# A paced feed-forward fill beside attention, and layers of neighbour jobs in turns behind it

## The chip, the cores and the metric

The kernel runs on one core of one Trainium2 chip. A core has five engines that run beside one another, each through its own list of instructions in order: TensorE (PE in the profile: matrix products, and transposes done as products), VectorE (DVE), ScalarE (ACT), GpSimd (POOL), and SyncE (SP), which here only issues DMAs. They wait for one another through semaphores. The metric is the device time of one execution in microseconds (us); lower is better.

## The reference

Masked attention on 8 batches of 8 heads with 576 positions of width 64, and behind it a feed-forward network on all 4608 tokens (512 wide, 2048 hidden):

```
scores = (1/8) * q @ k^T                      # 64 heads, 576x576
scores = where(scores >= rowmax - tau, scores, -1e9)
attn   = exp(scores - rowmax) / (sum + 1e-9)
x      = attn @ v                             # -> 4608 x 512
h      = x @ w_in                             # 512 -> 2048
g      = max(h, 0) + alpha * min(h, 0)
out    = g @ w_out                            # 2048 -> 512
```

The weights are float64, and single precision is wanted. So each operand is cut into a high part that TensorE takes whole and a low part with the rest, and a product is made of three (high by high, high by low, low by high).

## The kernel before

**Attention.** 32 pairs of heads, each cut into nine units (128 queries of a head; the fifth unit holds the rest of both heads). The main loop (L992) takes one unit a *cycle*, 288 cycles in all. In cycle i, PE makes the scores of unit i+2 (`s`, L423) and transposes the masked weights of unit i (`t`, `tk`, L467 and L483); DVE masks unit i (`p`, L458), takes the low part of a transposed unit (L523), and finds the row maxima of unit i+2 (`nmx`, L438); ACT makes exponentials and high parts. In four cycles of nine PE also multiplies weights by values (`av`, L570). A score tile has two homes in PSUM, so the scores of unit i+2 wait until unit i is masked. The finished x goes to DRAM (`xs`).

**The fill.** Feed-forward work is put into the same cycles. The first six of the 16 hidden chunks (`fcs1`) are done for *groups* of 256 tokens, 18 groups in all. A group's x is loaded and split (L698 to L705), then come six first-layer steps (L1 in this text: 12 products, `pha`), each followed a cycle later by the activation (L225 to L237), and then 36 second-layer products (L2, `acca`), which go into `part`. `Mlp.cycle` decides from a credit: each cycle adds `CYCLE` less the cycle's planned attention work, an L1 takes 1.31 and an L2 0.216, in planned microseconds. An L1 is let in while the credit is above `TH1` and the cycle has no `av`, an L2 while it is above `TH2`. Group x has one home, and a group's load enters the queue `l1` only behind the last L1 of the group before.

**Behind attention** (`behind`, L798). What is left of the groups becomes jobs of kind a; then nine jobs of 512 tokens for chunks 6 to 9 (kind b, `phb`, `accb`), then nine for chunks 10 to 15 (kind c, `phc`, `accc`). `order` lists whole steps: `step1` is one chunk's first layer, `step2` the whole second layer of 128 tokens. Between two jobs comes one `step1` of the next job, all `step2` of the last, then the other `step1`. x is loaded into `homexr` at the first step of the job before, and split in four quarters, one a step: ACT makes `homexh` (L868), DVE `homexl` (L869). Weights of later chunks are decoded from their float64 words in eight small steps each (`decode`, L826), among them POOL's product (L844) and its `join` (L162, recorded at L168).

All engine lists but SP's are in the order in which this code writes them.

Of the kernel before, what the change touches and what calls it, by code (L numbers as in the profile page):

```python
# [35 lines left out]
GB = 10  # L36
# [14 lines left out]
XO = 1  # L51
L2O = 3
P1 = 2
# [7 lines left out]
CYCLE = 2.6  # L61


def f(ap):
    return ap.bitcast(F32)
# [10 lines left out]
def tile_masked_attention_moe(  # L76
# [558 lines left out]
    def at_cycle(i, fn, *a):  # L635
        later.setdefault(i, []).append((fn, a))
# [44 lines left out]
    class Mlp:  # L681


        def __init__(self):
            self.l1, self.l2 = deque(), deque()
            self.acc = None
            self.live = 0
            self.gap = 0
            self.room = 0.0

        def ready(self, gi):
            t0, n = groups1[gi]
            st = {"g": {}}
            self.l1.append((gi, st, None))
            for i in range(F1):
                self.l1.append((gi, st, i))

        def step_l1(self, i):  # L698
            gi, st, fi = self.l1.popleft()
            t0, n = groups1[gi]  # L700
            if fi is None:
                st["xr"] = load_x(mem.mp1, t0, n, G1, 1)
                at_cycle(i + XO, lambda: st.update(x=split_x(mem.mp1, st["xr"], t0, n, G1, 1)))
                self.gap = i + XO + 2
                return  # L705
            name = f"a{gi}_{fi}"
            self.live += 1
            ph = layer1(ps_m, fcs1[fi], n, st["x"], name)

            def act(ph=ph):  # L710
                st[fi] = prelu1(mem.mp1, G1, fcs1[fi], n, ph, name, 2)
                prelu2(*st[fi], n)

            def spl():
                g = mem.mp1.tile([P, 2, G1], F32R, tag="g", name=f"g{name}", bufs=GB)
                split_g(g, st.pop(fi)[0], n, dict(p=nc.gpsimd, v=nc.vector).get(SPG))
                st["g"][fi] = g

            at_cycle(i + ACTO, act)
            at_cycle(i + SPLO, spl)  # L720
            if fi == F1 - 1:
                for o in range(0, n, P):
                    for fj in range(F1):
                        self.l2.extend((i + L2O, gi, st, o, fj, ti) for ti in range(3))

        def step_l2(self, i):
            _, gi, st, o, fj, ti = self.l2.popleft()
            t0, n = groups1[gi]
            m = min(P, n - o)
            if fj == 0 and ti == 0:  # L730
                self.acc = ps_m.tile([P, 512], F32, tag="pm", name=f"acca{gi}_{o}")
            acc = self.acc
            layer2(acc, fcs1[fj], st["g"][fj], o, m, fj == 0, fj == F1 - 1, (ti,))
            if ti < 2:
                return
            if o + P >= n:
                self.live -= 1
            if fj == F1 - 1:

                def put():  # L740
                    po = mem.mp1.tile([P, DM], F32, tag="po", name=f"po{gi}_{o}", bufs=1)
                    nc.scalar.activation(po[:m], acc[:m], AF.Copy)
                    nc.sync.dma_start(part[gi][o : o + m, :], po[:m])

                first_at_cycle(i + PUTO, put)

        def cycle(self, i, used, slot):

            self.room = min(self.room, TH3) + CYCLE - used
            l1 = False  # L750
            if self.l1 and i >= self.gap and self.live < GB:
                if self.l1[0][2] is None:
                    self.step_l1(i)
# [3 lines left out]
            while self.l2 and self.l2[0][0] <= i and self.l2[0][4] in self.l2[0][2]["g"] and ("o", fcs1[self.l2[0][4]]) in ready and self.room > TH2:  # L757
                self.step_l2(i)
                self.room -= 0.216
            return l1  # L760
# [37 lines left out]
    def behind():  # L798
# [5 lines left out]
        while mlp.l2 and (mlp.l2[0][4], mlp.l2[0][5]) != (0, 0):  # L804
            mlp.step_l2(10**6)
# [43 lines left out]
        class Job:  # L849


            def __init__(self, fcs, t0, n, gn, kind):
                self.fcs, self.t0, self.n, self.gn, self.kind = fcs, t0, n, gn, kind
                self.g, self.x, self.todo = {}, None, list(range(len(fcs)))
                self.tiles = list(range(0, n, P))
                self.name = f"{kind}{t0}"
# [7 lines left out]
            def split(self, c):  # L864
                n = self.n
# [17 lines left out]
            def step2(self, o):  # L883
                m = min(P, self.n - o)
                t = self.t0 + o
                if self.kind != "a":
                    pin = wpool.b.tile([P, DM], F32, tag="pin", name=f"pin{self.name}_{o}", bufs=3)
                    gi, r = divmod(t, G1)
                    nc.sync.dma_start(pin[:m], part[gi][r : r + m, :] if self.kind == "b" else part2[t // P][:m])
                acc = ps_2.tile([P, 512], F32, tag="acc", name=f"acc{self.name}_{o}", bufs=4)  # L890
                nf = len(self.fcs)
                for i, fc in enumerate(self.fcs):
                    layer2(acc, fc, self.g[i], o, m, i == 0, i == nf - 1)
                if self.kind == "a":
                    po = mem.mp1.tile([P, DM], F32, tag="po", name=f"po{self.name}_{o}", bufs=1)
                    nc.scalar.activation(po[:m], acc[:m], AF.Copy)
                    gi, r = divmod(t, G1)
# [3 lines left out]
                nc.vector.tensor_tensor(ob[:m], acc[:m], pin[:m], op=ALU.add)  # L901
                nc.sync.dma_start(part2[t // P][:m] if self.kind == "b" else out[t : t + m, :], ob[:m])

        olds = {}
        for gi, st, o, fj, ti in [x[1:] for x in mlp.l2]:
            if ti == 0 and fj == 0:
                job = olds.get(gi)
                if job is None:
                    t0, n = groups1[gi]
                    job = olds[gi] = Job(fcs1, t0, n, G1, "a")  # L910
                    job.tiles, job.todo, job.g = [], [], st["g"]
                job.tiles.append(o)
        for gi, st, fi in mlp.l1:
            job = olds.get(gi)
            if job is None:
                t0, n = groups1[gi]
                job = olds[gi] = Job(fcs1, t0, n, G1, "a")
                job.todo, job.g = [], st["g"]
                if fi is not None:
                    job.x = st["x"]  # L920
            if fi is not None:
                job.todo.append(fi)
        first = [olds[gi] for gi in sorted(olds)]
# [14 lines left out]
        ahead = {}  # L938
        for a, b in zip(jobs, jobs[1:]):
            k = next(i for i, x in enumerate(order) if x[0] is a)  # L940
            ahead.setdefault(k, []).append(b)

        weights = [[decode(fc, io) for io in "io" for fc in fcs] for fcs in (fa, fb)]
        nsteps = [sum(x[0].kind == c for x in order) for c in "ab"]
        starts = {}
        at_ = 0
        for ws, n, (lo, hi) in zip(weights, nsteps, ((0.0, 0.78), (0.1, 0.85))):
            for i, w in enumerate(ws):
                k = at_ + n * (lo + (hi - lo) * i / max(1, len(ws) - 1))
                for j, fn in enumerate(w):  # L950
                    starts.setdefault(int(k) + j, []).append(fn)
            at_ += n

        xq = deque()
        for k, (job, what, i) in enumerate(order):
# [3 lines left out]
            for b in ([job] if k == 0 and what == 1 else []) + ahead.get(k, []):  # L959
                if b.x is None:  # L960
                    while xq:
                        a, c = xq.popleft()
                        a.split(c)
                    b.load()
                    xq.extend((b, c) for c in range(NCC))
            if what == 1:
                while xq and xq[0][0] is job:
                    b, c = xq.popleft()
                    b.split(c)
                job.step1(i)  # L970
            else:
                job.step2(i)
            for fn in starts.get(k, []):
                fn()
            if xq:
                b, c = xq.popleft()
                b.split(c)
# [110 lines left out]
```

## Time and profile before

| | us |
|---|---|
| runs without profile (3) | 1440.97, 1444.02, 1445.97 |
| median | 1444.02 |
| the profiled execution | 1436.55 |
| its span, first to last instruction | 1434.7 |

Busy time: PE 94% of the span (8008 products), DVE 73%, ACT 59%, POOL 50%. Products are pipelined and their ends are modelled, so a busy PE is not always at its peak; the distance from one product's start to the next is the better measure. Attention with the fill runs until about 834 us, the a jobs until about 932 us, b jobs to about 1126 us, c jobs to the end.

The score tiles name the cycles: pair 26 begins at 665.3 us, pair 27 at 690.6, pair 28 at 716.3 (the first product of each pair's unit 0), pair 7 at 178.7 and pair 31 at 792.7. "Cycle 0" of a pair below is the one in which PE makes the scores of its unit 0.

### The profile page before, as it was taken

The numbers are of one execution on the slowest core, as the hardware profiler recorded it, in microseconds if no ns is written. First come the engines' busy times: TensorE is split into PE (matmuls) and PEld (weight loads), VectorE is DVE, ScalarE is ACT, GpSimd is POOL, SyncE is SP. The second block draws the span as 40 slices with busy tenths as digits, with TensorE's granted clock in tenths as the row PEclk, the third lists the DMA queues.
The fourth block names the chain that finished last, engine by engine and source line by source line (L and its number), as shares of the span: only waits on it lengthen the run. The fifth ranks groups of instructions, "written<-read, shape, count | busy, mean of one in ns | idle before, by whom it ended". The sixth has DMA issues, their size and how long they took to land.

```text
span 1434.7 us, 23581 instructions
## 1 busy us (share of the span) xinstructions
PE 1352.4 (94%) x8008; PEld 1181.1 (82%) x8008; DVE 1046.0 (73%) x2044; ACT 841.6 (59%) x1909; POOL 710.7 (50%) x834
## 2 busy tenths in 40 slices
PE   6998999999999999999999979989999999999998
PEld 4656888998998898899889867768888888888887
DVE  7988988988888888888888828647777644444432
ACT  7887988888888888888888733323233211121110
POOL 3884764665755666565665525514444322222221
PEclk9999999999999999999999989999999999999999
DMA  7645454544545535445454133434654522223221
GB/s 227 185 127 148 126 138 131 144 135 135 144 128 144 140 106 162 126 119 155 121 144 121 33 120 113 140 119 150 209 178 157 176 89 89 88 88 103 100 68 61
DMA packets 113448, 186.01 MB, mean 130 GB/s; under 512 B 16593, under 2 KB 47601, under 8 KB 113329
## 3 DMA queue, kind: packets, MB, share of 16 engines
q1 hardware_dynamic: 113328, 184.51, 43.0%
q8 instruction: 64, 1.05, 0.3%
q14 instruction: 56, 0.45, 0.1%
HBM read 104.41 MB, written 37.90 MB: 99 GB/s over the span
## 4 chain that ended last, share of the span: by engine, by line
PE 79%; DVE 9%; ACT 5%; issue 4%; POOL 2%; DMA 1%; SPq 0%; POOLq 0%; ACTq 0%; DVEq 0%
PE av L570 11%; PE s L423 11%; PE accc L243 10%; PE phc L213 10%; PE acca L243 8%; PE pha L213 7%; PE accb L243 7%; PE t L467 7%; PE phb L213 6%; DVE p L458 2%; DVE nmx L438 2%; PE tk L483 1%; DVE eo L523 1%; ACT eo L519 1%; POOL ga L237 1%
## 5 line engine op out<-in xcount | busy, mean ns | idle before, releaser
L438 DVE TENSOR_REDUCE nmx<-s 128x1 f32<-128x576 f32 x288 | 216.5, 752 | 77.7 <-PE s L423 75.3
L458 DVE SCALAR_TENSOR_TENSOR p<-s,thr,p 128x576 f32<-128x576 f32 x256 | 206.8, 808 | 3.1 <-ACT thr L451 2.6
L243 PE MATMUL acca<-wo,ga 128*128 128x512 f32 x648 | 199.4, 425 | 6.2 <-ACT ga L234 4.4
L423 PE MATMUL s<-kh,qst 128*128 128x288 f32 x640 | 145.2, 317 | 58.4 <-DVE p L458 44.2
L446 ACT ACTIVATE p<-s,nmx 128x576 f32<-128x576 f32 x256 | 190.3, 743 | 9.9 <-DVE nmx L438 9.7
L237 POOL TENSOR_TENSOR gc<-ptc,gc 128x512 fp32r<-128x512 f32 x54 | 69.9, 1294 | 216.8 <-ACT gc L234 216.8
L234 ACT ACTIVATE gc<-ptc 128x512 fp32r<-128x512 f32 x54 | 34.1, 632 | 237.5 <-DVE ptc L878 237.5
L423 PEld LDWEIGHTS s<-kh,qst 128*128 128x128 f32 x640 | 100.4, 193 | 88.6 <-issue 52.4
L467 PE MATMUL t<-ident,p 128*128 128x128 f32 x1024 | 156.4, 276 | 0.0
L243 PE MATMUL accc<-wo,gc 128*128 128x512 f32 x648 | 148.5, 389 | 0.0
L243 PEld LDWEIGHTS accc<-wo,gc 128*128 128x128 f32 x648 | 121.5, 188 | 25.5 <-POOL gc L237 0.3
L243 PEld LDWEIGHTS acca<-wo,ga 128*128 128x128 f32 x648 | 117.1, 195 | 27.5 <-ACT ga L234 6.3
L213 PE MATMUL pha<-xh,wi 128*128 128x256 f32 x672 | 136.1, 285 | 0.3 <-ACT pra L226 0.3
L213 PE MATMUL phc<-homexh,wi 128*128 128x512 f32 x432 | 134.6, 389 | 0.0
L423 PE MATMUL s<-kl,qst 128*128 128x288 f32 x640 | 134.3, 300 | 0.0
L467 PEld LDWEIGHTS t<-ident,p 128*128 128x128 f32 x1024 | 127.6, 142 | 0.1
L213 PEld LDWEIGHTS pha<-xh,wi 128*128 128x128 f32 x672 | 109.8, 190 | 4.6 <-ACT pra L226 1.2
L237 POOL TENSOR_TENSOR ga<-pta,ga 128x256 fp32r<-128x256 f32 x108 | 82.9, 768 | 57.5 <-ACT ga L234 50.4
L570 PE MATMUL av<-eo,vst 128*128 128x322 f32 (+1 forms) x512 | 107.9, 334 | 0.0
L869 DVE TENSOR_TENSOR homexl<-homexr,homexh 128x512 fp32r<-128x512 f32 (+1 forms) x88 | 69.5, 793 | 50.1 <-ACT homexh L868 50.1
L523 DVE TENSOR_TENSOR eo<-t,eo 128x512 fp32r<-128x512 f32 (+1 forms) x168 | 97.3, 592 | 9.3 <-ACT eo L519 9.0
L423 PEld LDWEIGHTS s<-kl,qst 128*128 128x128 f32 x640 | 103.5, 193 | 0.0
(146 smaller groups left out, 3234.3 us busy)
## 6 DMA issues: line engine op xcount, KB each, us to landing
kr<-in_k_dram SPq DMA_DIRECT2D x31, 320.0 KB
rb<-rvd SPq DMA_DIRECT2D x64, 144.0 KB
xs<-xa SPq DMA_DIRECT2D x32, 288.0 KB
pinb<-part SPq DMA_DIRECT2D x36, 256.0 KB
part<-obb SPq DMA_DIRECT2D x36, 256.0 KB
pinc<-part SPq DMA_DIRECT2D x36, 256.0 KB
out_dram<-obc SPq DMA_DIRECT2D x36, 256.0 KB
vr<-in_v_dram SPq DMA_DIRECT2D x28, 320.0 KB
```

The costliest lines, as they stand in the source:

```text
L213: nc.tensor.matmul(ph[:, :n], w[:, c, :], xx[:, c, :n], start=(c == 0 and ti == 0), stop=(c == NCC - 1 and ti == 2),)
L234: nc.scalar.activation(g[:, 0, :n], t[:, :n], AF.Copy)
L237: nc.gpsimd.tensor_tensor(g[:, 1, :n], t[:, :n], f(g[:, 0, :n]), op=ALU.subtract)
L243: nc.tensor.matmul(acc[:m, :], gg[:, g, o : o + m], w, start=(first and ti == 0), stop=(last and ti == 2))
L423: nc.tensor.matmul(ps[:, h, :288], w, kk[:, a + h * 288 : a + (h + 1) * 288], start=(ki == 0 and i == 0), stop=(ki == 1 and i == n - 1),)
L438: nc.vector.tensor_reduce(self.nmx[:, j : j + 1], self.S[u][0][:, :, :288], axis=AX.XY, op=ALU.max, negate=True)
L446: nc.scalar.activation(pj, ps[:, :, :288], AF.Exp, bias=nmx[:, j : j + 1], scale=1.0)
L458: nc.vector.scalar_tensor_tensor(pj, ps[:, :, :288], thr[:, j : j + 1], pj, op0=ALU.is_ge, op1=ALU.mult, accum_out=self.sm[:, c : c + 1])
L467: nc.tensor.transpose(tb[:, c, :], pt[:, j, j * D + c * P : j * D + (c + 1) * P], ident)
L523: nc.vector.tensor_tensor(dst[1], ps, f(dst[0]), op=ALU.subtract)
L570: nc.tensor.matmul(pa[:m, :n], w, x, start=(part == 0 and c == 0), stop=(part == z.parts[-1] and c == NKC))
L869: nc.vector.tensor_tensor(xl[:, c, :n], xr[:, c, :n], f(xh[:, c, :n]), op=ALU.subtract)
```

## The change

Five things change.

1. x of a group is loaded up to a group ahead (`prefetch`), split three cycles after its load, into two homes.
2. L2 products are held back: while a group's L1 steps are under way, `keep` leaves a reserve of six L2 for each L1 that is still to come, less `SLACK`; and between groups a reserve that grows with the cycles until the next group is ready. An L1 may also enter an `av` cycle when the credit is above 1.2.
3. `CYCLE` falls from 2.6 to 2.44; `GB`, the number of homes for g, rises to 11.
4. Behind attention a `step2` is one chunk of one 128-token tile, and the steps of two neighbour jobs take turns by their share of the job (from a to b jobs they don't).
5. There the x quarters and the weight decode are set by a clock of planned step costs (`event`), and POOL makes `homexl`.

On PE, in the cycles with the scores of units 2 and 3 of pair 27 (`s27_2`, `s27_3`; `t` and `tk` are transposes, `av26` weights by values), before:

```order
L423 MATMUL s27_2_9924<-kh27_9486,qst1_111 128x288 x2
L423 MATMUL s27_2_9924<-kl27_9488,qst1_111 128x288 x2
L467 MATMUL t27_0_9931<-ident_60,p27_0_9886 128x128 x4
L423 MATMUL s27_3_9961<-kh27_9486,qst1_111 128x288 x2
L423 MATMUL s27_3_9961<-kl27_9488,qst1_111 128x288 x2
L467 MATMUL t27_1_9967<-ident_60,p27_0_9886 128x128 x4
L483 MATMUL tk27_0_9972<-ident_60,p27_0_9886 128x128
L243 MATMUL acca10_0_9974<-wo0_944,ga10_0_9411 128x512 x3
L243 MATMUL acca10_0_9974<-wo1_1041,ga10_1_9457 128x512 x2
```

The same two cycles now:

```order
L425 MATMUL s27_2_9862<-kh27_9399,qst1_111 128x288 x2
L425 MATMUL s27_2_9862<-kl27_9401,qst1_111 128x288 x2
L469 MATMUL t27_0_9869<-ident_60,p27_0_9815 128x128 x4
L245 MATMUL acca9_0_9704<-wo1_1041,ga9_1_8847 128x512 x3
L245 MATMUL acca9_0_9704<-wo2_1146,ga9_2_9013 128x512 x3
L245 MATMUL acca9_0_9704<-wo3_1241,ga9_3_9135 128x512
L425 MATMUL s27_3_9904<-kh27_9399,qst1_111 128x288 x2
L425 MATMUL s27_3_9904<-kl27_9401,qst1_111 128x288 x2
L469 MATMUL t27_1_9910<-ident_60,p27_0_9815 128x128 x4
L485 MATMUL tk27_0_9915<-ident_60,p27_0_9815 128x128
L245 MATMUL acca9_0_9704<-wo3_1241,ga9_3_9135 128x512 x2
```

Seven L2 stand now in the first of the two cycles, where none stood, and two in the second in place of five.

On PE, behind attention, where the first layer of tokens 3584 and on begins (`pha3584_0`), before:

```order
L213 MATMUL pha3328_5_11936<-xh256_3328_11442,wi5_849 128x256 x2
L213 MATMUL pha3328_5_11936<-xl256_3328_11444,wi5_849 128x256
L213 MATMUL pha3328_5_11936<-xh256_3328_11442,wi5_849 128x256
L213 MATMUL pha3584_0_11966<-homexh0_11934,wi0_364 128x256
L213 MATMUL pha3584_0_11966<-homexl0_11932,wi0_364 128x256
```

And now:

```order
L215 MATMUL pha3328_5_11931<-xh256_3328_11089,wi5_849 128x256
L245 MATMUL acca3072_128_11920<-wo3_1241,ga12_3_11411 128x512 x3
L245 MATMUL acca3072_128_11920<-wo4_1335,ga12_4_11456 128x512 x3
L245 MATMUL acca3072_128_11920<-wo5_1473,ga12_5_11667 128x512 x3
L215 MATMUL pha3584_0_11968<-xh256_3584_11717,wi0_364 128x256
L215 MATMUL pha3584_0_11968<-xl256_3584_11719,wi0_364 128x256
```

Second-layer products of another group stand between the two first layers, and x of tokens 3584 and on comes from the fill's own second home (`xh256_3584`), not from `homexh0`.

On POOL, where b job 512 hands over to b job 1024 (`gb512_9` is the low part of the last g of the first, `wi10` a decoded weight, `rw2` the product of a decode), before:

```order
L237 TENSOR_TENSOR gb512_7_12975<-ptb512_7_12972,gb512_7_12975 128x512
L237 TENSOR_TENSOR gb512_8_12996<-ptb512_8_12993,gb512_8_12996 128x512
L237 TENSOR_TENSOR gb512_9_13017<-ptb512_9_13014,gb512_9_13017 128x512
L237 TENSOR_TENSOR gb1024_6_13040<-ptb1024_6_13037,gb1024_6_13040 128x512
L844 TENSOR_TENSOR rw2_11929<-rw2_11929 128x512
```

And now:

```order
L239 TENSOR_TENSOR gb512_8_12951<-ptb512_8_12948,gb512_8_12951 128x512
L869 TENSOR_TENSOR rw2_11828<-rw2_11828 128x512
L896 TENSOR_TENSOR homexl1_11829<-homexr_11832,homexh1_11830 128x512
L239 TENSOR_TENSOR gb512_9_12995<-ptb512_9_12992,gb512_9_12995 128x512
L170 TENSOR_TENSOR wi10_12925<-tw2_11825,rw2_11828 128x512
L896 TENSOR_TENSOR homexl1_11829<-homexr_11832,homexh1_11830 128x512
L239 TENSOR_TENSOR gb1024_6_13041<-ptb1024_6_13038,gb1024_6_13041 128x512
```

The last two x quarters of the next job stand now on POOL on either side of `gb512_9`, the last one behind the join of `wi10`.

The diff, cut to its core:

```diff
-GB = 10
+GB = 11
-XO = 1
+XO = 3
+SLACK = 6
+KEEP = 1.5
-CYCLE = 2.6
+CYCLE = 2.44
...
+        def prefetch(self, i):
+            if self.next >= len(self.groups) or self.next > self.cur + 1 or i <= self.split_at or mem.mp1 is None:
+                return
+            st = self.groups[self.next]
+            self.next += 1
+            xr = load_x(mem.mp1, st.t0, st.n, G1, 1)
+            def split():
+                st.x = split_x(mem.mp1, xr, st.t0, st.n, G1, 2)
+            at_cycle(i + XO, split)
+            self.split_at = i + XO
+            st.at = i + XO + 2
...
+        def keep(self, i):
+            if self.cur >= len(self.groups):
+                k = len(self.groups)
+                if k >= len(groups1):
+                    return 0
+                left = RDY + 9 * NPAIR * (-(-sum(groups1[k]) // S)) - i
+                return KEEP * max(0, left)
+            return 6 * (F1 - 1 - self.groups[self.cur].done) - SLACK
...
             self.room = min(self.room, TH3) + CYCLE - used
+            self.prefetch(i)
-                elif slot and self.room > TH1 and ("i", fcs1[self.l1[0][2]]) in ready:
+                if (slot and self.room > TH1 or self.room > 1.2) and ("i", fcs1[st.done]) in ready:
...
+            keep = self.keep(i)
+                if self.room <= TH2 or len(self.l2) <= keep:
+                    break
...
-                nc.vector.tensor_tensor(xl[:, c, :n], xr[:, c, :n], f(xh[:, c, :n]), op=ALU.subtract)
+                nc.gpsimd.tensor_tensor(xl[:, c, :n], xr[:, c, :n], f(xh[:, c, :n]), op=ALU.subtract)
...
-            s2 = [(a, 2, o) for o in a.tiles] if a else []
-            n = 0 if a and b and a.kind == "a" and b.kind == "b" else 1
-            order += s1[:n] + s2 + s1[n:]
+            s2 = [(a, 2, o, i) for o in a.tiles for i in range(len(a.fcs))] if a else []
+            turn = bool(a and b and a.kind == "a" and b.kind == "b")
+            both = []
+            for j, x in enumerate(s1):
+                share = 2 + j if turn else j / len(s1)
+                both.append((share, 0, len(both), x))
+            for j, x in enumerate(s2):
+                both.append(((j + 0.5) / len(s2), 1, len(both), x))
+            order += [x for *_, x in sorted(both, key=lambda y: y[:3])]
...
+        for a, b in zip([None] + jobs, jobs):
+            if b.x is not None or not b.todo:
+                continue
+            lo = max(free, begin.get(a, 0.0) if a else 0.0)
+            hi = max(begin[b] - 1.5, lo + 6.0)
+            event(lo, b.load)
+            for c in range(NCC):
+                event(lo + 5.0 + (hi - lo - 5.0) * (c + 0.5) / NCC, lambda b=b, c=c: b.split(c))
+            free = lo + 5.0 + (hi - lo - 5.0) * (NCC - 0.4) / NCC
```

## Rows read from the trace of the kernel before

**Rows 1.** The page's first line.

```profile
span 1434.7 us, 23581 instructions
```

**Rows 2.** PE's waits, whole span: who waited for whom; us in total, times, longest.

```profile
PE s L423 <- DVE p L458: 44.2, 43, 2.0
PE pha L213 <- ACT homexh L868: 9.1, 1, 9.1
...
PE acca L243 <- ACT ga L234: 4.4, 5, 1.1
...
PE phb L213 <- ACT homexh L868: 3.1, 2, 1.8
PE phb L213 <- DVE homexl L869: 1.5, 2, 0.9
PE acca L243 <- POOL ga L237: 1.4, 1, 1.4
```

**Rows 3.** PE's waits from 178.7 to 834 us.

```profile
PE s L423 <- DVE p L458: 29.9, 26, 2.0
```

**Rows 4.** Windows: us, busy us of each engine (instructions), granted PE clock, DMA share, GB/s.

```profile
178.70:792.70 614.00, 586.26 (x4225) 553.42 (x4224) 531.26 (x1177) 519.92 (x1237) 379.28 (x468) 0.99 0.48 134
665.30:690.60 25.30, 25.30 (x184) 23.97 (x183) 22.11 (x50) 21.21 (x52) 14.66 (x19) 1.00 0.45 127
690.60:716.30 25.70, 23.21 (x172) 21.83 (x171) 22.11 (x50) 22.15 (x53) 16.97 (x20) 1.00 0.52 146
834.10:951.70 117.60, 97.76 (x529) 81.01 (x527) 72.62 (x123) 40.50 (x87) 48.35 (x48) 0.92 0.37 119
```

**Rows 5.** PE in order of time, pair 27: start us, us, what, [idle before].

```profile
691.84 0.28 PE L213 MATMUL pha<-xh,wi 128*128 128x256 f32 x1
...
693.27 0.43 PE L423 MATMUL s<-kh,qst 128*128 128x288 f32 x2
...
694.27 0.48 PE L243 MATMUL acca<-wo,ga 128*128 128x512 f32 x1
695.66 0.54 PE L423 MATMUL s<-kh,qst 128*128 128x288 f32 x2 [0.91 <-DVE p L458]
...
698.48 0.51 PE L423 MATMUL s<-kh,qst 128*128 128x288 f32 x2 [1.58 <-DVE p L458]
...
699.55 1.41 PE L243 MATMUL acca<-wo,ga 128*128 128x512 f32 x5
700.80 0.63 PE L570 MATMUL av<-o,vst 128*128 128x256 f32 x4
...
701.97 0.69 PE L423 MATMUL s<-kh,qst 128*128 128x288 f32 x4
```

**Rows 6.** PE in order of time, pair 11, its units 0 and 3.

```profile
280.02 0.43 PE L423 MATMUL s<-kh,qst 128*128 128x288 f32 x2
...
288.43 0.50 PE L423 MATMUL s<-kh,qst 128*128 128x288 f32 x2 [2.01 <-DVE p L458]
```

**Rows 7.** The chain that ended last, from 949 us: start, us, what.

```profile
976.43 10.88 PE accb L243 x48
...
1156.00 16.32 PE accc L243 x72
```

**Rows 8.** Groups of instructions, whole span: count, busy us, mean ns, idle before.

```profile
L869 DVE TENSOR_TENSOR homexl<-homexr,homexh 128x512 fp32r<-128x512 f32 (+1 forms) x88 | 69.5, 793 | 50.1 <-ACT homexh L868 50.1
L237 POOL TENSOR_TENSOR gb<-ptb,gb 128x512 fp32r<-128x512 f32 x36 | 47.9, 1329 | 104.1 <-ACT gb L234 104.1
L877 DVE TENSOR_SCALAR ptb<-phb,alpha_sb 128x512 f32<-128x512 f32 x36 | 27.0, 750 | 37.9 <-PE phb L213 37.9
L878 DVE SCALAR_TENSOR_TENSOR ptb<-phb,ptb 128x512 f32<-128x512 f32 x36 | 24.9, 692 | 1.2
L234 ACT ACTIVATE gb<-ptb 128x512 fp32r<-128x512 f32 x36 | 22.8, 633 | 114.2 <-DVE ptb L878 114.2
L168 POOL TENSOR_TENSOR wo<-tw,rw 128x512 fp32r<-128x512 f32 x10 | 14.7, 1468 | 5.9 <-PE accb L243 5.8
```

More of the change, by code (lines that the diff above doesn't have):

```diff
@@ L803, in behind @@
             nready += 1
[L804 removed]
+        while mlp.l2 and (mlp.l2[0][3], mlp.l2[0][4]) != (0, 0):
             mlp.step_l2(10**6)
@@ L864, in split @@
             def split(self, c):
+                self.splits += 1
                 n = self.n
@@ L900, in step2 @@
                 ob = wpool.b.tile([P, DM], F32, tag="ob", name=f"ob{self.name}_{o}", bufs=3)
-                nc.vector.tensor_tensor(ob[:m], acc[:m], pin[:m], op=ALU.add)
+                nc.vector.tensor_tensor(ob[:m], acc[:m], self.pin[:m], op=ALU.add)
                 nc.sync.dma_start(part2[t // P][:m] if self.kind == "b" else out[t : t + m, :], ob[:m])
[L904 to L923, printed above, removed]
+        first = []
+        for st in mlp.groups:
+            if st.done == F1 and not any(x[1] is st for x in mlp.l2):
+                continue
+            job = Job(fcs1, st.t0, st.n, G1, "a")
+            job.todo = list(range(st.done, F1))
+            job.g, job.x, job.splits = st.g, st.x, NCC if st.x else 0
+            job.tiles = [o for o in range(0, st.n, P) if st.done < F1 or any(x[1] is st and x[2] == o for x in mlp.l2)]
+            first.append(job)
         ja = [Job(fa, t, min(G2, NT - t), G2, "b") for t in range(0, NT, G2)]
@@ new lines, in behind, with event @@
+        times, now = [], 0.0
+        begin, end = {}, {}
+        for x in order:
+            times.append(now)
+            if x[1] == 1:
+                begin.setdefault(x[0], now)
+            begin.setdefault((x[0], x[1]), now)
+            now += cost(x)
+            end[x[0]] = now
+        events = []
+        def event(t, fn):
+            events.append((t, len(events), fn))
+        weights = [[(fc, io) for io in "io" for fc in fcs] for fcs in (fa, fb)]
+        spans = ((0.0, begin[ja[0], 2] - 24.0), (begin[ja[1], 1], begin[jb[0], 1] - 30.0))
@@ new lines, in behind @@
+        last = -100.0
+        for ws, (lo, hi) in zip(weights, spans):
+            for i, (fc, io) in enumerate(ws):
+                t = lo + (hi - lo) * i / max(1, len(ws) - 1)
+                for j, fn in enumerate(decode(fc, io)):
+                    event(t + j * 2.4, fn)
+        free = 0.0
+        for a, b in zip([None] + jobs, jobs):
+            if b.x is not None or not b.todo:
+                continue
+            lo = max(free, begin.get(a, 0.0) if a else 0.0)
[4 more added lines that the diff above has]
+            free = lo + 5.0 + (hi - lo - 5.0) * (NCC - 0.4) / NCC
@@ L956, in behind @@
+        events.sort(key=lambda x: x[:2])
+        for k, x in enumerate(order):
+            job = x[0]
             if job.kind == "b" and wpool.b is None:
@@ L958, in behind @@
                 wpool.b = ctx.enter_context(tc.tile_pool(name="mp2", bufs=1, reuse_waits="tile"))
[L959 to L970, printed above, removed]
-            else:
[L972 to L977, printed above, removed]
+            while events and events[0][0] <= times[k]:
+                events.pop(0)[2]()
+            if x[1] == 1:
+                while job.x is None or job.splits < NCC:
+                    events.pop(0)[2]()
+                job.step1(x[2])
+            else:
+                job.step2(*x[2:])
     with tc.manual_schedule(engines=ENGINES) if ENGINES else ExitStack():
```

96 lines of the change are left out of this document (40 added, 56 removed).

## The prediction

> **What bounds the kernel now.** I read the page first, then PE's waits, then windows, then PE in order of time. The span is 1434.7 us [rows 1]; 1.85 us lie around it in the profiled execution of 1436.55 us. All sums below are made against that execution; the median of the runs lies 7.5 us above it, and the forecast is carried over by the difference. A change within 0.3% (4.3 us) is "the same" here.
>
> From about 952 us on, PE is never kept waiting: 48 products of 512 columns take 10.88 us and 72 take 16.32, both 0.2267 us a product, and so to the end [rows 7]. The 18 b and c jobs are 9 x 96 + 9 x 144 = 2160 such products, 490 us: nothing can be won there, only lost. What can be won lies before: in the fill, PE waits 29.9 us for a masked unit in 26 waits [rows 3], and behind attention 9.1 + 4.4 + 1.4 + 3.1 + 1.5 = 19.5 us for x quarters and g [rows 2].
>
> How attention is bound shows in two neighbour pairs. Pair 26 took 25.3 us with PE busy throughout; pair 27 took 25.7 us with 2.5 us of PE idle [rows 4]. Priced by rows: a cycle without fill is 1.00 us of PE (scores and transposes, 693.27 to 694.27), an `av` of 256 columns 1.17 us (700.80 to 701.97), so one of 322 columns 1.47 by its width, an L1 1.43 (691.84 to 693.27), an L2 0.25 (five from 699.55 to 700.80) [rows 5]. The fifth unit has four more score products of 288 columns, 0.53 us at the same rate. A pair without fill is then 9.0 + 0.53 + 2 x 1.17 + 2 x 1.47 = 14.8 us. Pair 26 has 3 L1 and 24 L2: 14.8 + 4.3 + 6.0 = 25.1, against 25.3 measured. Pair 27 has 3 and 12: 22.1, against 25.7. So 3.6 us of pair 27 are no work. They lie in its first three cycles: 2.4 us from 693.27 to 695.66 and 2.8 from 695.66 to 698.48, for 1.25 and 1.00 us of work [rows 5]. The fill had run dry there (the last group's L2 were done, the next x not split), and a cycle doesn't get shorter than about 2.4 us, since DVE and ACT have their own 22 us a pair [rows 4]. Elsewhere the pair is full, with cycles of up to 3 us. Two tight score homes let neither engine run ahead, so thin cycles don't pay back thick ones.
>
> **The change, part by part.**
>
> *The fill.* Counted from PE's list, cycles with one L2 or less and no L1 or `av` fall from 18 to 3 in pairs 7 to 30 (the three are in pair 10). In these 24 pairs L1 go from 72 to 71, L2 from 430 to 400. PE's work a pair is now 14.8 + 71/24 x 1.43 + 400/24 x 0.25 = 23.2 us, nearly the same in each pair. Two places can't be as short as that. First, cycles 0 to 2: in pair 26 they now hold 3 L1 and 2 L2, 3.0 + 4.3 + 0.5 = 7.8 us of PE. DVE has there, beside its usual masks and maxima, the reciprocals and two activations; pair 11, with an L1 in each of its first two cycles and a bare third, took 8.41 us from 280.02 to 288.43 with PE waiting 2.01 [rows 6]. I take that as the floor: 0.6 more. Second, cycle 5 now has 4 L2, 2.0 us, under the 2.4 us of the shortest row [rows 5]: 0.4 more. Pair 26 took 0.2 over its sum; I add that too. Forecast 24.4 us a pair, 586 us for 24 pairs in place of 614.0 [rows 4]: 28 us less. Bounds: 23.2 (PE's work alone) gives 57 less; 25.2 (the mean before, 614.0/24 = 25.6, less only the work taken away) gives 9 less. I stay nearest to the row of pair 11. Ahead of pair 7 two L1 fall away: 1 us less.
>
> *The smaller credit* moves 3 L1 and 28 L2 behind attention (82 and 456 before, 79 and 428 now). There they are plain PE work: 3 x 1.43 + 28 x 0.2267 = 10.7 us more.
>
> *x ahead, in two homes.* The loads and splits are as many as before. The load goes to SP a group earlier and waits for nothing that isn't long done: its raw home is free once the last split has run. ACT's and POOL's part of the split stood in the dry cycles and now falls into full ones, on engines with 3 and 10 us to spare a pair [rows 4]. I cost it at nothing, covered by that; uncovered it would be one ACT operation before the exponential in one cycle of nineteen, at most 1 us a group, 12 us in all, inside the bound of 25.2.
>
> *Behind attention, up to 952 us.* The 9.1 us go whole: tokens 3584 on now find x in the fill's second home, and the first x that must be loaded there is wanted some 30 us later. The 5.8 us for g go: a g is now wanted only when the next job's turns come. The granted clock over the stretch is 0.92 [rows 4], up to 9 us of lost products, some of them inside the waits; I take 7 now, 4 after. Between a jobs the last x quarter stands on POOL behind the last g. At half the widths of [rows 8] that chain is about as long as the six L2 and the ten products that cover it: 0 to 0.6 us, 2 in all three.
>
> *The hand-overs with POOL in them.* In the b and c jobs the last quarter of the next x stands behind the last g of this job. From the end of that g's products: DVE 0.75 and 0.69, ACT 0.63, POOL 1.33 for the low part and 1.33 for the quarter [rows 8], with 0.3 for the passing on: 5.0 us. PE meanwhile does twelve L2 and ten products of the next job: 22 x 0.2267 = 5.0 us. So a plain hand-over costs nothing to 0.1 us. In five of the eight b hand-overs a piece of weight decode, 1.47 us for a join [rows 8], stands between, as shown on POOL for job 512: 1.5 us each, 7.5 us. The eight c ones are plain: 0.8 us with three b ones at most 1.1.
>
> The Trainium skill, GPSIMD Engine Reference, section 4.1 (Engine selection), speaks against the move: it has elementwise work with two inputs on VectorE, and GpSimd about half as fast. The trace agrees in kind: 0.79 us on DVE, 1.33 on POOL for the same 128x512 [rows 8]. By a full factor of two the two POOL operations would take 3.2 us in place of 2.7, and sixteen hand-overs 8 us more. The row's figure stands in the sum.
>
> *From b job 0 to b job 512* there is no covering L2. Before, PE waited 3.1 + 1.5 us there [rows 2]. Now three quarters and a join stand between `gb0_8` and `gb0_9` on POOL, and one quarter behind: from the end of that layer 3.7 us to the low part of `gb0_8`, then 5 x 1.33 + 1.47 = 8.1, so 11.8 us, and PE wants it at 5.0: 6.8 us of wait.
>
> Sum for this stretch and the hand-overs: before 19.5 + 7 = 26.5; now 6.8 + 2 + 7.5 + 1 + 4 = 21. It gives 5 us. Bounds: 18 less (only job 512's wait left), 25 more (below).
>
> *GB* 11 in place of 10 and the shorter second-layer steps issue nothing new. Nothing, in both directions.
>
> **Sum.** -28 - 1 + 10.7 - 5 = -23.5 us. 1436.55 becomes 1413; with the 7.5 us to the median, 1420 us.
>
> **The rivals.**
>
> *DVE and ACT set the pace (16%).* DVE and ACT are busy 22 us of 25.5 in every pair [rows 4], and in the dry cycles PE was already waiting for DVE. If a pair doesn't fall under 25.2, attention gives 9, and the sum is -9 - 1 + 10.7 - 5 = -4: 1439 us, at the border of the same. Against it: pair 26 itself ran with no wait at 25.3 on more PE work, so its floor isn't shown to be that high.
>
> *DVE keeps up everywhere (15%).* Its floor in cycles 0 to 2 may be pair 11's own; with 23.6 us a pair (0.4 over the work) attention gives 48, the sum is -43: 1401 us.
>
> *The hand-overs lead: slower (9%).* If every one of the sixteen costs a decode piece's 1.5 us, and PE's clock falls behind each as it fell between 834 and 952 us (0.92 granted, about 7 us for some ten waits [rows 2, 4]; say 1.7 us each, a wait's length of half rate), they cost 16 x 3.2 = 51 in place of 8.5, and the sum is +19: 1463 us. It decides from 2.0 us a hand-over on, where the 23.5 us won are spent. For it: the b and c stretch has no wait at all now, and its cover is equal to the chain within 0.1 us. Against it: DVE loses 88 splits of 0.79 us, so the chain's first half can only become quicker.
>
> *The fill doesn't hold (5%).* If `keep` only shifts the dry cycles, attention gives nothing, and 10.7 - 5 = +6: 1450 us. PE's list with 3 bare cycles for 18 speaks against it.
>
> **How the numbers follow.** The forecast has the other 55%, with a range of its own of 1408 to 1432 (24.0 to 24.9 us a pair). The full range takes in most of the fast rival and the border one: 1398 to 1442; the two slower cases and the far end of the fast one, under 20%, stay out. Faster: 55 + 15 and a little over half of the border case, 80%. The same: 7%. Slower: 9 + 4 and a rest of the border case, 13%.
>
> **What would show it.** Right: PE's waits for the masked unit between pair 7 and the end fall from 29.9 to about 15 us, the rest sitting before unit 3 of a pair; pairs of 24.4 us, all alike; no wait of 9 us behind attention; a wait of 5 to 8 us before `phb512_6`; waits for `homexl` of 1 to 2 us before the first layers of five b jobs, none in the c jobs. Wrong: pairs still of 25 us or more (DVE's floor), waits for POOL in all c jobs (hand-overs mis-sized), or a clock under 0.95 after 952 us.

## The result, and the profile after

The changed kernel took 1428.4 us (median of four runs, 1426.9 to 1433.5), the kernel before 1445.0 beside it: a ratio of 0.9895, 95% interval 0.9863 to 0.9928. A second set of runs gave 0.9923 (0.9894 to 0.9952). That is 11 to 15 us faster by these ratios; 1420 was forecast, with 1398 to 1442 as the range. The kernel before moves between 1435 and 1448 from run to run, so kernels are compared by their ratios below. The profiled execution of before was one of its short ones (1436.55) and that of after the longest of its four (1433.48), so the two traces differ by 3 us only; a second profile of after, of 1425.2 us span, is used beside the first.

The page's first line of after [rows 1], and PE's waits over the whole span (who waited for whom; us in total, times, longest) [rows 2]:

```profile
span 1431.7 us, 23496 instructions
```

```profile
PE s L425 <- DVE p L460: 18.3, 20, 2.4
PE phb L215 <- POOL homexl L896: 14.5, 10, 1.9
...
PE pha L215 <- ACT pra L228: 2.9, 12, 0.5
PE pha L215 <- POOL homexl L896: 2.9, 4, 1.2
PE t L469 <- DVE e L525: 2.5, 2, 1.8
...
PE phc L215 <- POOL homexl L896: 0.7, 1, 0.7
```

The 9.1 us for x and the 5.8 for g are gone, and 18.1 us for POOL's low part of x have come. At the c hand-overs (where one job's products give way to the next's) only one wait of a product is long enough for the list, but the weight loads ahead of these products (PEld) wait at all nine:

```profile
PEld phc L215 <- POOL homexl L896: 4.7, 9, 1.1
```

From 184.2 to 820 us, the stretch of [rows 3], the wait for the masked unit shows what is left of 29.9 us:

```profile
PE s L425 <- DVE p L460: 3.3, 3, 2.1
```

Windows of after, with the columns of [rows 4]: pairs 7 to 30, pairs 10, 18, 26 and 27 alone, pair 31 to the first b product, the b jobs, the c jobs:

```profile
184.20:778.80 594.60, 582.00 (x4183) 541.85 (x4182) 530.34 (x1176) 517.05 (x1235) 377.94 (x467) 1.00 0.50 139
257.13:284.34 27.21, 23.28 (x159) 21.73 (x158) 21.93 (x49) 23.00 (x54) 17.37 (x18) 0.94 0.54 147
455.69:482.71 27.02, 24.74 (x172) 22.50 (x171) 21.74 (x49) 22.90 (x54) 17.39 (x18) 1.00 0.57 158
655.69:680.16 24.47, 24.19 (x183) 22.98 (x182) 22.35 (x51) 22.41 (x54) 18.56 (x23) 1.00 0.54 152
680.16:704.73 24.57, 24.33 (x171) 22.23 (x170) 21.71 (x49) 20.91 (x52) 13.03 (x17) 1.00 0.47 130
778.80:910.60 131.80, 128.04 (x810) 115.14 (x809) 82.35 (x157) 61.92 (x143) 78.16 (x92) 0.99 0.29 96
910.60:1119.50 208.90, 194.17 (x817) 156.00 (x816) 121.00 (x164) 61.91 (x109) 123.25 (x97) 0.97 0.47 155
1119.50:1427.90 308.40, 307.49 (x1345) 251.40 (x1343) 103.93 (x148) 51.19 (x87) 112.26 (x88) 1.00 0.29 94
```

Pairs 26 and 27 took 25.3 and 25.7 us before [rows 4] and take 24.5 and 24.6 now. Pairs 10 and 18 show what still fails; pair 10 holds all three bare cycles (cycles with next to no fill) that PE's list has left there. The b and c jobs, which took 193.2 and 305.0 us, take 208.9 and 308.4.

What stands at a b hand-over shows on POOL (start, us, what, in brackets the idle time before) from the last g of b job 512:

```profile
951.98 1.30 POOL L239 TENSOR_TENSOR gb<-ptb,gb 128x512 fp32r<-128x512 f32 x1 [1.89 <-ACT gb L236]
953.23 1.75 POOL L170 TENSOR_TENSOR wi<-tw,rw 128x512 fp32r<-128x512 f32 x1
954.93 1.45 POOL L896 TENSOR_TENSOR homexl<-homexr,homexh 128x512 fp32r<-128x512 f32 x1
```

and on PE, which takes up that quarter:

```profile
956.44 0.50 PE L215 MATMUL phb<-homexl,wi 128*128 128x512 f32 x1 [1.81 <-POOL homexl L896]
```

This is the forecast's chain (last g, then the last quarter) with a join in it. At job 2048 POOL has no piece between, but there DVE is late: PE ended the last layer of job 1536 at 996.55, and DVE took it up 2.06 us later, behind two pieces of decode:

```profile
997.05 1.18 DVE L147 SCALAR_TENSOR_TENSOR tw<-rw,tw 128x512 int32<-128x512 int32 x1
998.27 0.43 DVE L152 TENSOR_SCALAR rw<-tw 128x512 int32<-128x512 int32 x1
998.61 0.75 DVE L904 TENSOR_SCALAR ptb<-phb,alpha_sb 128x512 f32<-128x512 f32 x1
```

So each of the seven hand-overs from 1024 on waits: 1.81, 0.98, 1.56, 1.86, 0.98, 1.56 and 1.87 us, three behind a join, two behind POOL's other decode product (L869, 1.04 us), two behind DVE's pieces.

### The profile page after: what moved, and what is told of

Same layout as the page of the kernel before. It is cut to its first block, busy times and chain, and to the rows that moved or that the text cites. A ratio compares the mean times of both kernels' runs of the same rounds, so it can differ in the third digit from the quotient of the medians.

```text
span 1431.7 us, 23496 instructions
## 1 busy us (share of the span) xinstructions
PE 1364.2 (95%) x8008; PEld 1179.7 (82%) x8008; DVE 992.6 (69%) x1959; ACT 839.2 (59%) x1906; POOL 805.9 (56%) x913
## 4 chain that ended last, share of the span: by engine, by line
PE 76%; ACT 10%; DVE 6%; POOL 3%; issue 2%; DMA 2%; SPq 1%; ACTq 0%; DVEq 0%; POOLq 0%
PE phc L215 10%; PE accc L245 10%; PE s L425 10%; PE av L572 10%; PE acca L245 9%; PE pha L215 8%; PE t L469 6%; PE accb L245 6%; PE phb L215 5%; DMA xr<-xs 1%; ACT p L448 1%; POOL homexl L896 1%; DVE p L460 1%; ACT kh L352 1%; ACT xb L585 1%
## 5 line engine op out<-in xcount | busy, mean ns | idle before, releaser
L245 PE MATMUL acca<-wo,ga 128*128 128x512 f32 x648 | 193.4, 415 | 0.2 <-DVE eo L525 0.2
L904 DVE TENSOR_SCALAR ptc<-phc,alpha_sb 128x512 f32<-128x512 f32 x54 | 40.6, 752 | 169.2 <-PE phc L215 169.2
L245 PE MATMUL accc<-wo,gc 128*128 128x512 f32 x648 | 154.8, 389 | 0.0
L215 PE MATMUL pha<-xh,wi 128*128 128x256 f32 x720 | 149.4, 290 | 4.5 <-ACT pra L228 2.9
L245 PEld LDWEIGHTS accc<-wo,gc 128*128 128x128 f32 x648 | 121.7, 188 | 25.5
L215 PE MATMUL phc<-homexh,wi 128*128 128x512 f32 x432 | 141.8, 389 | 0.0
L215 PEld LDWEIGHTS pha<-xh,wi 128*128 128x128 f32 x720 | 119.4, 193 | 11.4 <-ACT pra L228 7.7
L245 PE MATMUL accb<-wo,gb 128*128 128x512 f32 x432 | 107.7, 399 | 0.0
L236 ACT ACTIVATE gb<-ptb 128x512 fp32r<-128x512 f32 x36 | 22.8, 633 | 143.6 <-DVE ptb L905 143.6
```

The costliest lines, as they stand in the source:

```text
L215: nc.tensor.matmul(ph[:, :n], w[:, c, :], xx[:, c, :n], start=(c == 0 and ti == 0), stop=(c == NCC - 1 and ti == 2),)
L236: nc.scalar.activation(g[:, 0, :n], t[:, :n], AF.Copy)
L245: nc.tensor.matmul(acc[:m, :], gg[:, g, o : o + m], w, start=(first and ti == 0), stop=(last and ti == 2))
L904: nc.vector.tensor_scalar(t[:, :n], ph[:, :n], 0.0, alpha_sb[:, fc : fc + 1], op0=ALU.min, op1=ALU.mult)
```

## The experiments

One table for all. A ratio is to runs of before in the same set. The stretches are read from PE in order of time, in one trace of each kernel: where pair 7 starts, pairs 7 to 30, pair 31 to the first b product, and what the b and c jobs take above 2160 products of 0.2267 us (489.7 us).

| kernel | ratio to before | median us | pair 7 at | pairs 7–30 | 31 to b | b, c above |
|---|---|---|---|---|---|---|
| before | 1 | 1438 to 1445.5 | 178.7 | 614.0 | 140.0 | 8.5 |
| after | 0.9895 (0.9863–0.9928) | 1428.4 | 184.2 | 594.6 | 131.8 | 27.6 |
| after_again | 0.9923 (0.9894–0.9952) | 1430.0 | 180.5 | 593.2 | 130.3 | 27.8 |
| fill_alone | 0.9816 (0.9786–0.9845) | 1413.2 | 179.7 | 594.1 | 134.7 | 8.1 |
| behind_alone | 1.0099 (1.0066–1.0132) | 1454.0 | 179.0 | 618.5 | 134.2 | 26.6 |
| credit_alone | 0.9830 (0.9800–0.9859) | 1416.9 | 179.9 | 591.4 | 141.8 | 9.1 |
| low_on_dve | 0.9940 (0.9916–0.9965) | 1431.8 | 181.2 | 592.4 | 135.6 | 22.4 |
| quarters_early | 0.9709 (0.9682–0.9735) | 1398.3 | 180.3 | 591.9 | 126.8 | 4.2 |
| no_reserve | 0.9881 (0.9848–0.9913) | 1421.2 | 182.5 | 591.5 | 127.3 | 25.1 |
| x_two_later | 0.9918 (0.9892–0.9943) | 1427.8 | 180.1 | 591.6 | 134.6 | 27.2 |
| turns_early_alone | 0.9878 (0.9856–0.9901) | 1428.9 | 180.0 | 621.1 | 130.4 | 2.6 |
| credit_and_early | 0.9681 (0.9661–0.9701) | 1399.1 | 179.0 | 591.4 | 129.7 | 4.2 |
| early_no_reserve | 0.9651 (0.9633–0.9669) | 1394.6 | 181.7 | 591.6 | 124.1 | 2.6 |
| early_credit_back | 0.9780 (0.9761–0.9798) | 1413.3 | 179.8 | 617.4 | 115.5 | 2.6 |

**The two halves, and the credit.** In `fill_alone` the class `Job` and all behind it is that of before, the fill that of after; in `behind_alone` the other way round. `credit_alone` is the kernel before with

```
-CYCLE = 2.6
+CYCLE = 2.44
```

fill_alone: 

> The new fill (x ahead, reserve, credit 2.44, 11 g) with the old order behind attention. Theory: the gain sits in attention; behind attention the traces show 22.0 us of PE waits before and 22.4 after, so the new turns there give 0 to 5 us. Then this kernel takes 1428 to 1434 us, and its trace keeps the 9 us wait or something like it behind attention, with no waits in the b and c jobs. Rival: the turns behind attention carry the gain and the fill only pays for the three L1 and 28 L2 that it moves there; then 1441 us or more.

behind_alone: 

> The old fill with the new order behind attention (turns, low part on POOL). Theory: 1440 to 1446 us, since seven b hand-overs wait 10.6 us for POOL where before the a jobs waited 9.1 and 5.8 us. Rival (the turns carry the gain): 1433 us or less. The pairs 7 to 30 should take 614 us as before in either case.

credit_alone: 

> The kernel before with one number changed: CYCLE 2.44 in place of 2.6. In PE's list the bare cycles of pairs 7 to 30 (at most one L2, no L1, no av) fall from 21 to 2 by that alone, and 2 L1 and 15 L2 items move behind attention. Theory A (what counts is that no cycle is bare, whoever sees to it): pairs of about 24.5 to 24.8 us, 1429 to 1435 us. Theory B (the reserve and the x ahead do it; the credit only moves work behind attention at 1.43 and 0.23 us each, 6 us): 1443 us or more.

after_again: 

> The changed kernel once more, unedited, for a second profile: its first profile was its slowest run (1433.48) and that of the kernel before a run below all its others (1436.55), so stretches of the two traces differ by 3 us where the medians differ by 16.6. Expected: 1428 us; if the scatter sits in attention, pairs 7 to 30 take 585 to 592 us here where the first profile has 594.6; if it sits ahead of pair 7 (28.2 us in pair 6, granted clock halved there), pair 7 starts near 179 us where the first has 184.2.

The fill alone is 1.8% faster than before, more than the whole change; the half behind attention alone is 1.0% slower. All stood in one set of runs: from `fill_alone` to `after_again` 16.8 us are lost. Both theories on `fill_alone` and `behind_alone` were too kind to the turns. And one number, the credit, does what the fill does: pairs 7 to 30 of `credit_alone` are as short as any, and its 1416.9 us lie below even theory A's range. Its window, and PE's longest waits in it:

```profile
179.90:771.30 591.40, 581.43 (x4174) 542.26 (x4173) 530.98 (x1174) 516.18 (x1234) 374.16 (x459) 0.99 0.50 139
```

```profile
PE s L423 <- DVE p L458: 5.3, 6, 1.6
PE pha L213 <- ACT pra L226: 2.6, 11, 0.3
```

The second profile of after places the scatter: pair 7 starts at 180.5 where the first had 184.2, pairs 7 to 30 differ by 1.4 us, the b and c jobs by 0.2. So the scatter of after sits ahead of pair 7, and the shortfall in the pairs is none of it. The kernel before scatters in the pairs: up to pair 31 `behind_alone` and `turns_early_alone` (below) have the very list of before on PE, and their pairs 7 to 30 took longer than its 614.0 us, at a lower granted clock than its 0.99:

```profile
179.00:797.50 618.50, 590.59 (x4224) 557.27 (x4224) 531.50 (x1177) 519.13 (x1237) 379.27 (x468) 0.98 0.48 133
180.00:801.10 621.10, 593.33 (x4225) 559.77 (x4223) 531.47 (x1177) 519.93 (x1237) 378.44 (x468) 0.98 0.48 132
```

Against these the new fill takes 24 to 28 us off the pairs, where the profile of before gives 19 to 21.

**Why the b jobs wait: the engine or the place.** `low_on_dve` and `quarters_early` each edit one line of the changed kernel:

```
-                nc.gpsimd.tensor_tensor(xl[:, c, :n], xr[:, c, :n], ...
+                nc.vector.tensor_tensor(xl[:, c, :n], xr[:, c, :n], ...
```

```
-            hi = max(begin[b] - 1.5, lo + 6.0)
+            hi = max(begin[b] - 6.0, lo + 6.0)
```

low_on_dve: 

> The changed kernel with one word edited: behind attention the low part of x goes back to DVE. In the b and c jobs the changed kernel loses 27.7 us against 0.2267 us a product (6.5 before phb512_6, 13.3 in the seven later b hand-overs, 3.4 in the c ones). Theory A (the wait is POOL's own queue: last g, join and quarter stand in a row): on DVE the chain from the last layer's end is 0.75 + 0.69 + 0.63 + 0.62 + 0.79 + 0.3 = 3.8 us against 5.0 us of cover, later only where a decode piece of 1.4 to 1.8 us stands on DVE; 10 to 14 us lost in place of 27.7, so 1413 to 1418 us. Rival B (the turns put the last quarter too late whichever engine does it): 1425 us or more, with phb waiting for DVE in place of POOL.

quarters_early: 

> The changed kernel with one number edited: the quarters of the next x are spread up to 6.0 us ahead of the next job in place of 1.5, still on POOL. In POOL's list the last quarter then stands ahead of the last g in the b hand-overs, with the join behind that g. Theory A: what costs is the quarter's place behind the last g and the join; the seven b waits and the 0.3 of the c hand-overs go and only the one before phb512_6 stays: 8 to 11 us lost in place of 27.7, 1410 to 1416 us. Rival B (POOL simply has too much to do at a hand-over: then the last g comes 1.3 us or a join later and accb waits for it instead): 1422 us or more.

The place, in the main. With the low part on DVE the b and c jobs lose 22.4 us (the c jobs next to nothing, at 305.1 us), and the stretch ahead of them takes 5 more than in `after_again`. At job 2048 of `low_on_dve` the high part is late already, since on ACT it stands behind the last g too, and the low part after it; ACT, POOL and DVE, and PE:

```profile
997.15 0.63 ACT L236 ACTIVATE gb<-ptb 128x512 fp32r<-128x512 f32 x1 [5.21 <-DVE ptb L905]
997.69 0.61 ACT L895 ACTIVATE homexh<-homexr 128x512 fp32r<-128x512 f32 x1
```

```profile
997.86 1.28 POOL L239 TENSOR_TENSOR gb<-ptb,gb 128x512 fp32r<-128x512 f32 x1 [4.73 <-ACT gb L236]
998.33 1.35 DVE L896 TENSOR_TENSOR homexl<-homexr,homexh 128x512 fp32r<-128x512 f32 x1 [1.27 <-ACT homexh L895]
```

```profile
998.35 0.50 PE L215 MATMUL phb<-homexh,wi 128*128 128x512 f32 x1 [2.05 <-ACT homexh L895]
999.74 0.50 PE L215 MATMUL phb<-homexl,wi 128*128 128x512 f32 x1 [0.88 <-DVE homexl L896]
```

DVE's price failed as well: 0.79 us in the expectation, 1.35 here, beside POOL's product of the last g. Of the 72 such subtractions in this trace the 12 with POOL idle beside them took 0.68 to 0.69 us, the other 60 from 0.81 to 1.78, 1.36 in the median.

With the quarters early, on POOL, the last quarter stands ahead of the last g of job 512 and the join behind it:

```profile
933.59 1.29 POOL L896 TENSOR_TENSOR homexl<-homexr,homexh 128x512 fp32r<-128x512 f32 x1
935.52 1.29 POOL L239 TENSOR_TENSOR gb<-ptb,gb 128x512 fp32r<-128x512 f32 x1 [0.64 <-ACT gb L236]
936.77 1.76 POOL L170 TENSOR_TENSOR wi<-tw,rw 128x512 fp32r<-128x512 f32 x1
```

All the waits of the b and c jobs go but those before `phb512_6`; the kernel is 2.9% faster than before, at 1398.3 us well below theory A's range. Its windows (pair 31 to the first b product, b, c), and all of PE's waits from 772 us on:

```profile
772.20:899.00 126.80, 125.55 (x811) 113.64 (x809) 82.67 (x157) 62.05 (x143) 79.74 (x92) 1.00 0.31 99
899.00:1088.10 189.10, 187.32 (x818) 154.12 (x817) 122.39 (x164) 61.97 (x109) 125.77 (x98) 0.99 0.54 172
1088.10:1392.90 304.80, 304.76 (x1345) 252.03 (x1343) 103.92 (x148) 50.86 (x86) 110.94 (x87) 1.00 0.29 95
```

```profile
PE phb L215 <- POOL homexl L896: 1.8, 2, 1.5
PE pha L215 <- ACT po L754: 0.9, 1, 0.9
PE pha L215 <- POOL homexl L896: 0.4, 1, 0.4
```

POOL's work in the b jobs is as in after (125.77 us against 123.25), so it never was too much for POOL. The Trainium skill's rule is to keep such work on VectorE (GPSIMD Engine Reference, section 4.1, Engine selection). On the late quarter that engine was worth 5.4 us in the b and c jobs and nothing in the whole (0.9940 beside 0.9923), the place 23.6 us on POOL. Early quarters with the low part on DVE were not run, so which engine is better once nothing waits is not shown.

**The reserve and the x ahead.** One edit each of the changed kernel:

```
-            keep = self.keep(i)
+            keep = 0
```

```
-XO = 3
+XO = 5
```

no_reserve: 

> The changed kernel without the reserve: second-layer steps are no longer held back (keep is 0). In PE's list there is then 1 bare cycle in pairs 7 to 30 (3 with the reserve). Theory A (the credit does the pacing and the reserve hardly anything): pairs 7 to 30 take 590 to 596 us, the time is 1425 to 1433 us. Rival B (the reserve is what carries the fill over a batch's end): bare cycles and pairs of 25.7 us come back, 1436 us or more.

x_two_later: 

> The changed kernel with XO 5 in place of 3: the split of x stands five cycles behind its load in place of three. Theory A (at a batch's end ACT waits in order for a load that has not landed, 0.85 to 2.15 us, and its exponential behind it): pairs 6, 10, 14 and 18, which took 26.9, 27.2, 25.7 and 26.1 us, come to about 25; 10 L2 items more go behind attention (2.3 us); 1423 to 1428 us. Rival B (these pairs are long because the fill is starved there, whatever the split's place): the pairs stay at 26 to 27 and the time is 1429 to 1433 us.

Without the reserve the pairs take 591.5 us: theory A, though the 1421.2 us lie below its range. Beside `after_again` 3.0 us less lie between pair 31 and the b jobs and 2.7 in the b and c jobs. Pair 10, with no bare cycle left in it, takes 24.8 us in place of 27.2, and pair 11 25.2 in place of 24.2. As to x, the long pairs of after begin at a batch's end, where a group becomes ready and its load goes out at once. On ACT in pair 18 (start, us, what, idle before):

```profile
467.40 0.38 ACT L585 ACTIVATE xb<-av 64x256 f32<-64x256 f32 x1
469.93 1.06 ACT L201 ACTIVATE xh<-xr 128x1024 fp32r<-128x1024 f32 x1 [2.15 <-DMA xr<-xs]
471.01 0.60 ACT L521 ACTIVATE e<-t 128x512 fp32r<-128x512 f32 x1
471.50 0.73 ACT L448 ACTIVATE p_t<-s,nmx 128x576 f32<-128x576 f32 x1
```

SP issued that load at 463.81, and ACT, in order, waited for it, with `e` behind, for which PE then waited 1.8 us. With XO 5 no split waits for its load, and pairs 6, 10, 14 and 18 come from 26.9, 27.2, 25.7 and 26.1 us to 25.7, 25.4, 25.0 and 25.1. But pairs 7, 11, 15 and 19 grow by 0.6 to 1.2 each, the sum of 7 to 30 falls by 1.6 us only, one L1 and four L2 more are left for behind pair 30, where pair 31 to the b jobs takes 134.6 us in place of 130.3, and the time doesn't move. Theory A had the mechanism and not its worth.

**Put together.** `turns_early_alone` is `behind_alone` with -6.0 in place of -1.5 as above; `credit_and_early` is that with the credit 2.44; `early_no_reserve` and `early_credit_back` are `quarters_early` with `keep = 0` and with the credit 2.6.

turns_early_alone: 

> The old fill (credit 2.6) with the new order behind attention and its quarters spread up to 6.0 us ahead. With the quarters late the same kernel was 1.0% slower than before. Theory A (the turns are good once the quarter stands ahead of the last g and the join): from pair 31 to the end 625 to 630 us in place of 638.2 before and 650.5 with late quarters (the 9 to 10 us wait for the x of 3584 stays, since the old fill brings it no x), 0.5 to 1% faster than before. Rival B (the turns themselves lose time and only the new fill hid it): 638 us or more from pair 31 on, no faster than before.

credit_and_early: 

> The kernel of turns_early_alone with the credit 2.44: none of the new fill's code, only its smaller credit. Theory A (two things carry the gain: no bare cycles, by the credit, and no late quarter): pairs 7 to 30 take 590 to 594 us, 1398 to 1405 us, that is up to 5 us behind quarters_early (1398.3) for the x of 3584, which the old fill doesn't bring ahead. Rival B (the reserve and the x ahead carry several us more once the hand-overs are clean): 1408 us or more.

early_no_reserve: 

> quarters_early without the reserve. Theory A: the 7 us that no_reserve was faster than the changed kernel lie ahead of the b jobs (127.3 us from pair 31 to the first b product against 130.3, two us in attention) and are there with early quarters too in part: 1392 to 1397 us. Rival B (the two gains are the same waits behind attention, already gone with early quarters): 1397 to 1400 us.

early_credit_back: 

> quarters_early with the credit back at 2.6, reserve and x ahead kept. In PE's list 8 L1 and about 50 L2 items more then stand in attention (about 24 us of PE) and 10 cycles of pairs 7 to 30 are bare in place of 3. Theory A (pairs are bound by PE's work plus bare cycles): pairs 7 to 30 take about 615 us, behind attention 23 us less, together 1397 to 1403 us. Rival B (full cycles are bound by DVE and ACT, so more fill costs nothing there): pairs stay near 593 and the kernel takes 1385 us or less. Rival C (bare cycles are what cost): over 1408 us.

The new order behind attention is good once the quarter is early (its turns, its clock of planned costs and POOL's part were not tried one by one): 1.2% faster than before on the old fill, 622.6 us from pair 31 to the end where before had 638.2, though the pairs took 621.1 us at a granted clock of 0.98. With the credit added, `credit_and_early` is at 1399.1: beside `quarters_early` the rest of the new fill (x ahead, reserve) is worth nothing that can be told. Without the reserve it may be worth something: `early_no_reserve`, in the same set as `credit_and_early` and 4.5 us under it (the intervals of the two ratios overlap), is at 1394.6 us the fastest of all, 3.5% under before. Its windows of the same three stretches show PE at full clock and all but never idle:

```profile
773.30:897.40 124.10, 123.26 (x795) 111.48 (x794) 83.99 (x155) 61.30 (x141) 79.19 (x91) 1.00 0.32 101
897.40:1084.90 187.50, 185.74 (x818) 153.01 (x817) 122.28 (x164) 61.97 (x109) 125.50 (x98) 1.00 0.54 174
1084.90:1389.70 304.80, 304.76 (x1345) 252.11 (x1343) 103.92 (x149) 50.85 (x86) 110.82 (x87) 1.00 0.29 95
```

With the credit back at 2.6 attention takes 25.5 us more, as theory A had it (617.4 us against about 615), but only 12.9 come back behind it: PE now waits 6.2 us there, for an x whose load went out at 843.2 us and whose split began at 849.2, and from pair 31 to the b jobs the granted clock is 0.96 in place of 1.00. That less second-layer work is left to cover this x is likely, and not shown. The wait:

```profile
PE pha L215 <- ACT homexh L895: 6.2, 1, 6.2
```

So the time fell to rival C's side (1413), with theory A's mechanism in attention.

## Why the prediction came out as it did

The direction and the range held; the size was 8 us too good in the runs (14 to 20 in the traces), and the errors had both signs: from pair 31 to the b jobs and before `phb512_6` the change did better than forecast, in the pairs, ahead of them and at the other hand-overs worse. That the range held owes something to its width (44 us around a forecast of some 24 less). By its own steps, against the profile of before, forecast first, then the first and the second profile of after:

- **Pairs 7 to 30, 28 us less: 19.4 and 20.8.** The mechanism was right, and an undisturbed pair takes 24.5 us where 24.4 were forecast; against the two longer traces of the same list the 28 nearly come out. But the split was wrong: PE is busy 582.0 us there, 24.25 a pair in place of the 23.2 priced by rows, and waits 12.6 in place of 29; for the masked unit it waits 3.3 us from pair 7 on where about 15 were to be left. (The same prices give 566 us for the list of before, where PE was busy 586.26.) Wrong in kind was the reason: the forecast booked the credit as a loss of 10.7 us and the gain to the paced fill. The credit alone empties the list of bare cycles (2 in place of 21, by the looser count of its expectation, which takes up to three second-layer products for bare) and gives 22.6 us.
- **x ahead, nothing: at most some 2 us.** ACT waited 3.7 and 1.7 us for x in the two profiles; without these waits (`x_two_later`) the pairs are 1.6 us shorter and the time is the same. The text named the place (ACT's split before an exponential) but priced it as an operation, not as a wait of up to 2.15 us for a load that has not landed.
- **Ahead of pair 7, 1 less: 5.5 and 1.8 more.** Pair 6 takes 26.9 to 28.2 us in place of 25.0, beside the first such group.
- **From pair 31 to the b jobs, 5.2 less (the moved 10.7 included): 8.2 and 9.7.** The 9.1 us wait went as forecast: with the old fill 10.3 us of it stand in `turns_early_alone`, with the new one none in `fill_alone`.
- **`phb512_6`, a wait of 6.8: 3.9.** In four pieces, of which the longest are 1.57 and 1.50. Behind them, from 925.2 to 935.5 us, the clock was granted at half, the lower of its two levels, and the products stand 0.427 us apart in place of 0.2267; with these, 8.9 us are lost there, and 8.1 were before.
- **The other hand-overs, 7.5 + 1 us: 14.8 in the seven b ones, 3.3 in the nine before c jobs.** (The 6.5, 13.3 and 3.4 us in the expectation of `low_on_dve` leave out some 4 us of slowed products.) The step that failed is "a plain hand-over costs nothing to 0.1 us". The five with a piece of decode on POOL lose 8.9 us where 7.5 were forecast: 2.1 behind each join, 1.25 behind the smaller product of L869, which was priced as a join. But the two b ones that are plain on POOL lose 6.0: the forecast missed the pieces on DVE ahead of the last layer's first step, which make the g itself late. And each wait costs 0.3 us beyond itself: in the c jobs the chain of 5.0 us came out as priced, ended just behind its cover, the products that PE has meanwhile, and 0.3 us are lost at eight of the nine, 0.95 at one. Waits for POOL in all c jobs were among the prediction's signs of being wrong, and the weight loads show them.

The rival in which the hand-overs lead was the nearest on this half: 18.1 us over sixteen is 1.1 a hand-over, a little over half its point of decision. The forecast never asked what would happen if the quarter stood 4.5 us earlier, though its own sum (chain 5.0, cover 5.0) said that the place decided.

Not settled: why dropping the reserve gives some 3 us between pair 31 and the b jobs, of which 2.1 may be one L1 and three L2 done earlier, and why pairs 6, 10, 14 and 18, once shorter, leave the next pair longer.

## What to carry to other kernels

A change of two halves is to be priced and, where that can be, run in halves: here -1.8% and +1.0% made a -1.0% that looked like a small win. At a hand-over write down, on every engine in order, what is queued ahead of the piece that the next stage wants, small pieces of other work among them, and move the wanted piece ahead before moving it to another engine. A price read from rows holds for what ran beside those rows: look whether that changes too. Where a budget per slot overdraws now and pays back in empty slots, try the budget alone before building machinery around it.

## What was not expected of the hardware

A wait of PE costs more than its length: at the c hand-overs the first product behind a wait takes 0.50 us in the trace in place of 0.39, and 0.3 us are lost even where the wait itself is too short to be listed. With 13 us less of idle PE in the b jobs the granted clock there was 0.99 and 1.00 in place of 0.97. And one operation on DVE or POOL has no one price. DVE's subtraction for x, 128x512, took 0.67 to 0.69 us in the 40 of 72 cases of before in which POOL was idle beside it, and 1.34 to 1.37 in the 11 beside POOL's product of the last g (L237) alone. POOL's join (L170) took 1.29 us in after with DVE idle beside it (one case) and 1.74 to 1.75 beside DVE's decode pieces L147 and L152 (three). That POOL's other work was what stretched DVE's was read from which instructions overlap, not tried by a run of its own.
